# A fused block-sparse attention and SwiGLU kernel: where the later query masks are made, which PSUM bank three tiles use, and what is loaded ahead of the down weights

## The chip, the cores and the metric

The kernel runs on one core of a Trainium2 chip. The metric is the device time of one execution in microseconds, as a median of several runs; lower is better. Besides those runs, one execution was profiled, and all details of where time goes come from it.

Engines are named as in the profile: PE (matrix multiply; PEld is its weight load), DVE (vector), ACT (scalar), POOL (GpSimd), SP (the queue that issues most plain DMAs and the DMA transposes). Each engine runs its instructions in the order of the program, and so do the queues that issue DMAs.

## The reference

```python
# q, k, v: [4, 8, 768, 64]; sampled_blocks: [24, 3]
scores = (q @ k^T) / sqrt(64)
# block mask over 24 blocks of 32: neighbours within 1, first and last block in rows and columns,
# and three sampled key blocks for each query block; outside the mask the score is -1e9
attn = exp(scores - max); attn = attn / sum(attn)
x = (attn @ v)            # heads side by side: [3072, 512]
xn = x / sqrt(mean(x*x) + 1e-6) * rms_g
out = (silu(xn @ w_gate) * (xn @ w_val)) @ w_out      # d_ff = 1536
```

The same mask serves all batches and heads. All heads of a token must be done before its norm and its feed-forward part (FFN) can start.

## The kernel before

**Tiling.** The query columns are cut into groups: batch 0 in three groups of two 128-query chunks, batches 1 to 3 in two groups of three chunks each. For each group the kernel loops over the eight heads: `scores` (L316) multiplies keys by queries into a PSUM tile `st` and lets ACT take the exponential into `ex`; `values` (L332) multiplies `ex` by the values, with a column of ones that gives the row sums; `pv` and `pv_two` (the latter for group 0, two heads in a tile) divide by the sum and write to `stage`. The values of a head are computed one head later than its scores (`late_pv`, L518).

**The mask** is part of the matmul: 24 more rows (`D:KR`) of `KT` hold an indicator of the key's block, and 24 more rows of `QT` hold a large negative number where the block isn't allowed. The rows for the queries of group 0 (`qmask[:, 0:2P]`) are made by DVE at L237. Those for groups 1 and 2 are made by DVE in the middle of group 0: `qnat` at L641, then `mask_queries` twice (L246, L650), and then SP sends them to the other seven heads (L652).

**From a group to its FFN.** When a group's last head is done, `squares` (L364) sums the squares on DVE, `rms_power` (L374) takes the power -0.5 on POOL (`rstd`), `rms_scale` scales rows into `xs` on DVE, and `transpose_x` turns them on PE (`tx`) and copies them to `xg` on DVE. For some later groups a DMA turns them; of group 2 one chunk is turned by PE, in tile `tx3` (L412). Then `ffn_pieces` (L426) makes a list of pieces: 12 gates (`gp`), 12 values (`vp`) and the down parts (`yp`, which read `wo`). The pieces are handed out over the next group's heads at fixed places (`position`, L500), four a head, so PE's order is written out in the program.

**PSUM.** `ps_f` has three banks (tag `ff`) for FFN tiles, fillers and some transposes. `ps_o` has one bank (tag `ot`) for value tiles and other transposes. `ps_s` has two double banks for `st`.

**Loads.** Nearly all loads are issued by POOL, in program order: keys, queries and values of batch 0, with the later query chunks (`load_q0(pr, 2, NC)`, tile `qbf`), `load_gv` for `wg` and `wv` in a first quarter, a second quarter and a half, then `wo` (L636), then from group 1 on batch 1's pairs (`load_qk`, `load_v`, L537). `rms_power` stands in the same queue. Batch 0's keys and queries are turned by PE (`transpose_qk`, tile `tqk`); those of later batches by DMA on SP (`turn`, L297, tile `turned`), and placed by two more DMAs a step later (`place`, L305). For batch 1, `turn` starts with group 2 (L583).

**Fillers.** `keep_busy` (L167) issues matmuls on a constant tile whose result nobody reads.

Of the kernel before, what the change touches and what calls it, by code (L numbers as in the profile page):

```python
# [9 lines left out]
FP32 = mybir.dt.float32  # L10
BF16 = mybir.dt.bfloat16
# [7 lines left out]
def kernel(  # L19
# [17 lines left out]
    nc = tc.nc  # L37
# [100 lines left out]
    rmsg = const.tile([P, NP], FP32, name="rmsg")  # L138
    gain = const.tile([P, DM], FP32, name="gain")

    def first_cast(h, which):
        cols = 2 * D if which else NC * D
        t16 = ld.tile([P, cols], BF16, name="t16", tag=f"t16{which}", bufs=1)
        nc.scalar.copy(out=t16, in_=first[(h, which)][:, 0:cols])
        return t16

    def first_turn(src, which, unread=None):
# [40 lines left out]
    for pr in range(NP):  # L188
        if pr == 0:
            load_q0(1, 0, 2)  # L190
        elif pr + 1 < NP:
            load_one(0, pr + 1, kbf)
            load_q0(pr + 1, 0, 2)
        load_v(0, pr)
        if pr == NP - 2:
            load_q0(0, 2, NC)
    load_gv(0, NF // 4)
    load_q0(1, 2, NC)
    load_gv(NF // 4, NF // 2)

    mhalf = const.tile([P, HC], FP32, name="mhalf")
    nc.vector.memset(mhalf, -0.5)
# [34 lines left out]
    for m, (lo, hi) in enumerate(((0, 6), (6, 11), (11, 16))):  # L237
        nc.vector.tensor_scalar(
            out=qmask.rearrange("p (c i r) -> p c i r", c=NC, r=16)[:, 0:2, :, lo:hi],
            in0=bm[0:NB, :].rearrange("p (i m) -> p i m", m=3)[:, :, m].unsqueeze(1).unsqueeze(  # L240
                3).to_broadcast([NB, 2, 8, hi - lo]),
            scalar1=-MASKV, scalar2=MASKV, op0=ALU.mult, op1=ALU.add)
    mask_keys(0, HC)
    qnat = const.tile([32, S], BF16, name="qnat")

    def mask_queries(third):  # L246

        lo, hi = 2 * third, 2 * third + 2
        nc.vector.tensor_copy(
            out=qmask.rearrange("p (c r) -> p c r", c=NC)[:, lo:hi, :],  # L250
            in_=qnat[0:NB, :].rearrange("p (r c) -> p c r", c=NC)[:, lo:hi, :])

    def copy_rows(T, m, lo, hi, c_lo, c_hi):

        nc.vector.tensor_copy(
# [20 lines left out]


    def transpose_qk(b, pr, which, lo, hi, spare, copy):
# [61 lines left out]
    def pv(grp, h, ex, stage):  # L340
        n = grp[2]
        op = ps_o.tile([P, HC, 80], FP32, name="op", tag="ot")
        values(grp, h, ex, op)
        rz = work.tile([P, HC], FP32, name="rz", tag="rz", bufs=2)
        nc.vector.reciprocal(out=rz[:, 0:n], in_=op[:, 0:n, D])  # L345
        nc.vector.tensor_tensor(  # L346
            out=stage[:, 0:n, h * D:(h + 1) * D], in0=op[:, 0:n, 0:D],
            in1=rz[:, 0:n].unsqueeze(2).to_broadcast([P, n, D]), op=ALU.mult)

    pair_op = {}  # L350

    def pv_two(grp, h, ex, stage):

        if h % 2 == 0:
            pair_op[0] = ps_o.tile([P, 2, 2, 80], FP32, name="op2", tag="ot")
        op = pair_op[0]
        values(grp, h, ex, op[:, h % 2])
        if h % 2 == 0:
            return
        rz = work.tile([P, 2, 2], FP32, name="rz2", tag="rz2", bufs=2)  # L360
        nc.vector.reciprocal(out=rz, in_=op[:, :, :, D])
        nc.vector.tensor_tensor(  # L362
            out=stage[:, 0:2, (h - 1) * D:(h + 1) * D].rearrange("p c (e d) -> p e c d", e=2),
            in0=op[:, :, :, 0:D], in1=rz.unsqueeze(3).to_broadcast([P, 2, 2, D]), op=ALU.mult)  # L364
# [36 lines left out]
    def transpose_x(e, half):  # L401
        xs, xg, n = e["xs"], e["xg"], e["grp"][2]
        if by_dma(e):
            if e["grp"] == groups[FIRST] and half == 2:
                t = ps_o.tile([P, KD, P], BF16, name="tx3", tag="ot")
                for c in range(KD):
                    nc.tensor.transpose(
                        out=t[:, c, :], in_=xs[:, 2, c * P:(c + 1) * P], identity=ident)
                nc.vector.tensor_copy(out=xg[:, :, 2 * P:3 * P], in_=t)
            return  # L410
        if half == 2:
            return  # L412
        pool, tag = (ps_f, "ff") if e["grp"] == groups[0] else (ps_o, "ot")
        t = pool.tile([P, 2, HC, P], BF16, name="tx", tag=tag)
        for w in range(2):
            c = 2 * half + w
            for it in range(n):
                nc.tensor.transpose(  # L418
                    out=t[:, w, it, :], in_=xs[:, it, c * P:(c + 1) * P], identity=ident)
# [87 lines left out]
    waiting = []  # L507
    ending = None

    def after_pv(e, h):  # L510
# [7 lines left out]
    def late_pv():  # L518

        e, h, ex = waiting.pop(0)  # L520
        if e["grp"] == groups[0]:
# [6 lines left out]
                    squares(e, it, (H - 2) * D, H * D)  # L528
                rms_power(e)
        else:  # L530
            pv(e["grp"], h, ex, e["stage"])
            after_pv(e, h)
        return e if h == H - 1 else None

    def side_work(gi, h):

        if gi == 1:  # L537
            if h == 1:
                load_qk(1, 0)
                load_v(1, 0)  # L540
                load_v(1, 1)
                load_qk(1, 1)
            if h == 3:
                nc.gpsimd.dma_start(
                    out=gain, in_=moe_rms_g.unsqueeze(0).to_broadcast([P, DM]))
                load_qk(1, 2)
            if h == 5:
                load_qk(1, 3)
# [41 lines left out]
    TX = 2  # L590

    def begin(grp):
        return {
# [5 lines left out]
    def first_group():  # L599
# [24 lines left out]
        keep_busy(1, 512)  # L624
        copy_rows(KT, kind, 2, 4, 0, S)
        copy_rows(QT, qmask, 2, 4, 0, 2 * P)
        k_turn(1)
        q_turn(1, (act, act))
        keep_busy(1, 512)

        head(1, lambda: keep_busy(1, 512))
# [1 line left out]
        load_q0(2, 2, NC)  # L633
        load_q0(3, 2, NC)
        load_gv(NF // 2, NF)
        nc.gpsimd.dma_start(out=wo, in_=moe_w_out.rearrange("(c p) f -> p c f", p=P))  # L636
        k_turn(2)

        head(2, lambda: q_turn(2))
        late_pv()  # L640
        nc.vector.tensor_scalar(  # L641
            out=qnat[0:NB, :].rearrange("p (a w) -> p a w", w=32),
            in0=bm[0:NB, :].unsqueeze(2).to_broadcast([NB, NB, 32]),
            scalar1=-MASKV, scalar2=MASKV, op0=ALU.mult, op1=ALU.add)
        keep_busy(1, 512)

        head(3)
        late_pv()
        cast_v(0, 1, nc.vector)
        for third in range(1, FIRST):  # L650
            mask_queries(third)
        nc.sync.dma_start(  # L652
            out=QT[0][D:KR, 1:H, 2 * P:S],
            in_=qmask[:, 2 * P:S].unsqueeze(1).to_broadcast([NB, H - 1, S - 2 * P]))
        k_turn(3)
        keep_busy(1, 512)

        head(4, lambda: q_turn(3))
        late_pv()
# [3 lines left out]
        late_pv()  # L663
        cast_v(0, 2, nc.vector)
        transpose_qk(0, 0, 1, 1, HC, True, (dve, dve))
        keep_busy(1, 512)

        head(6)
        late_pv()
# [5 lines left out]
        keep_busy(1, 512)  # L675

        head(7)
        late_pv()
        keep_busy(1, 512)
        late_pv()  # L680
# [2 lines left out]
    for gi, grp in enumerate(groups):  # L683
# [6 lines left out]
        for h in range(H):  # L690
# [42 lines left out]
            if h == 0 and ending is not None:  # L733
                rms_scale(ending, 0)
            if h == H - 1:
                squares(cur, 1, 0, (H - 1) * D)
            waiting.append((cur, h, ex))
    pe = waiting[0][0]
    squares(pe, 2, 0, (H - 1) * D)
# [48 lines left out]
```

## Time and profile before

| | |
|---|---|
| median of 3 runs | 313.87 us (313.78 to 314.47) |
| the profiled execution | 314.58 us, of which the span from first to last instruction is 312.8 us |
| granted TensorE clock | 1.000 |
| PE busy | 302.8 us, 97% |
| DVE, ACT, POOL busy | 202.7, 205.1, 52.9 us |
| DMA, POOL's queue | 17.90 MB |
| DMA, SP's queue | 18.47 MB |
| first values of group 0's FFN (`gp`) | at 27.1 us |
| first down part (`yp`) | at 46.25 us |
| first scores of batch 1 (384 columns) | at 68.6 us |

A row of the profile that names an engine, a line and `out<-in` tells the tiles by the program's names. "x12" counts instructions. In a wait "A <- B", A stood still and B ended that. The end of a matmul is modelled, so a busy PE can still be late.

### The profile page before, as it was taken

The numbers are of one execution on the slowest core, as the hardware profiler recorded it, in microseconds if no ns is written. First come the engines' busy times: TensorE is split into PE (matmuls) and PEld (weight loads), VectorE is DVE, ScalarE is ACT, GpSimd is POOL, SyncE is SP. The second block draws the span as 40 slices with busy tenths as digits, with TensorE's granted clock in tenths as the row PEclk, the third lists the DMA queues.
The fourth block names the chain that finished last, engine by engine and source line by source line (L and its number), as shares of the span: only waits on it lengthen the run. The fifth ranks groups of instructions, "written<-read, shape, count | busy, mean of one in ns | idle before, by whom it ended". The sixth has DMA issues, their size and how long they took to land.

```text
span 312.8 us, 7261 instructions
## 1 busy us (share of the span) xinstructions
PE 302.8 (97%) x2850; PEld 201.1 (64%) x2869; DVE 202.7 (65%) x557; ACT 205.1 (66%) x332; POOL 52.9 (17%) x79
## 2 busy tenths in 40 slices
PE   8888999999999999999999999999999999999996
PEld 5666886976787566655666566655666566655653
DVE  6978875775578647682767457683777636674860
ACT  4976775777788586667676766766767567632331
POOL 9935132100220122012010122010000100010000
PEclk9999999999999999999999999999999999999999
DMA  7999999999789469605784277714000130002002
GB/s 166 271 210 208 208 265 142 175 227 136 209 147 162 104 134 158 141 20 146 149 152 101 70 182 127 143 40 119 34 2 0 36 118 2 1 2 101 2 0 102
DMA packets 66730, 36.84 MB, mean 118 GB/s; under 512 B 48308, under 2 KB 62288, under 8 KB 66696
## 3 DMA queue, kind: packets, MB, share of 16 engines
q0 software_dynamic: 16064, 17.90, 31.7%
q1 hardware_dynamic: 50596, 18.47, 27.7%
q8 instruction: 22, 0.36, 0.5%
q14 instruction: 12, 0.10, 0.1%
q10 hardware_dynamic: 36, 0.01, 0.0%
HBM read 28.59 MB, written 6.29 MB: 112 GB/s over the span
## 4 chain that ended last, share of the span: by engine, by line
PE 86%; DMA 7%; ACT 3%; DVE 2%; issue 1%; SPq 1%; ACTq 0%
PE yp L464 19%; PE gp L436 19%; PE vp L447 18%; PE st L325 18%; PE op L336 11%; DMA turned<-qbf 4%; ACT ex L328 2%; DMA QT<-turned 2%; DMA first<-in_q_dram 1%; PE tx L418 0%; DVE QT L293 0%; DVE junk L369 0%; DVE stage L362 0%; PE tqk L288 0%; SPq L133 0%
## 5 line engine op out<-in xcount | busy, mean ns | idle before, releaser
L328 ACT ACTIVATE ex<-st 128x768 bf16<-128x768 f32 x192 | 153.9, 812 | 56.2 <-PE st L325 54.5
L325 PE MATMUL st<-QT,KT 88*128 88x384 bf16 (+1 forms) x432 | 93.5, 308 | 1.9 <-DMA QT<-turned 0.7
L451 DVE SCALAR_TENSOR_TENSOR u<-th,gp 128x384 bf16<-128x384 bf16 (+1 forms) x108 | 54.8, 508 | 40.7 <-ACT th L440 39.0
L436 PE MATMUL gp<-xg,wg 128*128 128x384 bf16 (+1 forms) x432 | 80.7, 307 | 0.0
L447 PE MATMUL vp<-xg,wv 128*128 128x384 bf16 (+1 forms) x432 | 80.2, 307 | 0.4 <-DVE u L451 0.4
L464 PE MATMUL yp<-wo,hps 128*128 128x512 bf16 (+1 forms) x284 | 71.6, 369 | 0.9
L440 ACT ACTIVATE th<-gp 128x384 bf16<-128x384 f32 (+1 forms) x108 | 48.9, 453 | 28.9 <-PE gp L436 28.7
L453 DVE TENSOR_TENSOR hps<-u,vp 128x384 bf16<-128x384 bf16 (+1 forms) x108 | 55.1, 510 | 11.4 <-PE vp L447 0.3
L325 PEld LDWEIGHTS <-KT 88*128 88x128 bf16 x432 | 41.7, 98 | 27.0 <-issue 1.9
L447 PEld LDWEIGHTS <-wv 128*128 128x128 bf16 x432 | 40.6, 97 | 20.9 <-issue 0.6
L436 PEld LDWEIGHTS <-wg 128*128 128x128 bf16 x432 | 40.2, 97 | 20.3
L336 PEld LDWEIGHTS <-ex 128*128 128x128 bf16 x1152 | 46.0, 98 | 11.2 <-DVE stage L362 0.8
L336 PE MATMUL op<-Vp,ex 128*128 128x65 bf16 x1152 | 48.8, 194 | 1.6 <-DVE stage L362 0.5
L464 PEld LDWEIGHTS <-hps 128*128 128x128 bf16 x300 | 27.7, 97 | 22.4
L377 POOL TENSOR_TENSOR rstd<-ssq,mhalf 128x3 f32<-128x3 f32 (+1 forms) x9 | 7.3, 815 | 139.4 <-DVE ssq L369 139.4
L345 DVE RECIPROCAL rz<-op 128x3 f32<-128x3 f32 (+1 forms) x64 | 11.2, 174 | 26.2 <-PE op L336 26.1
L470 ACT ACTIVATE yo<-yp 128x512 f32<-128x512 f32 (+1 forms) x25 | 14.4, 576 | 16.0 <-PE yp L464 16.0
L99 POOL DMA_DIRECT2D vraw<-in_v_dram x16 | 12.0, 753 | 69.4 <-DVE Vp L118 60.4
L346 DVE TENSOR_TENSOR stage<-op,rz 128x192 bf16<-128x192 f32 (+1 forms) x64 | 21.8, 341 | 2.2
L369 DVE CUSTOM_DVE_ANT_0 junk<-stage 128x448 bf16<-128x448 bf16 (+1 forms) x24 | 14.8, 618 | 0.6
L389 DVE SCALAR_TENSOR_TENSOR xs<-stage,rstd,gain 128x512 bf16<-128x512 bf16 x15 | 10.4, 748 | 4.4 <-POOL rstd L377 4.4
L87 POOL DMA_DIRECT2D kbf<-in_k_dram x15 | 11.1, 742 | 7.0 <-DMA wo<-in_moe_w_out_dram 7.0
(73 smaller groups left out, 104.6 us busy)
## 6 DMA issues: line engine op xcount, KB each, us to landing
vraw<-in_v_dram POOLq DMA_DIRECT2D x16, 384.0 KB, 5.1
out_dram<-yo SPq DMA_DIRECT2D x23, 256.0 KB, 2.2
kbf<-in_k_dram POOLq DMA_DIRECT2D x15, 192.0 KB, 5.8
qbf<-in_q_dram POOLq DMA_DIRECT2D x12, 192.0 KB, 6.0
KT<-turned SPq DMA_DIRECT2D x24, 96.0 KB, 4.2
QT<-turned SPq DMA_DIRECT2D x24, 96.0 KB, 2.3
wo<-in_moe_w_out_dram POOLq DMA_DIRECT2D x1, 1536.0 KB, 20.5
wg<-in_moe_w_gate_dram POOLq DMA_DIRECT2D x2, 384.0 KB, 9.8
```

What stands on the lines that cost most here:

```text
L325: nc.tensor.matmul(out=at[:, e, 0:tg], lhsT=KT[b % 2][0:KR, h, jt * P:(jt + 1) * P], rhs=QT[b % 2][0:KR, h, c0 * P:c0 * P + tg], start=Tru ...
L328: nc.scalar.activation(out=ex[:, nj * part:nj * (part + 1), :], in_=at[:, 0:nj, 0:tg], func=AF.Exp, scale=SCALE)
L336: nc.tensor.matmul(out=op[:, it, 0:VW], lhsT=ex[:, jt, it * P:(it + 1) * P], rhs=Vp[b % 2][:, h, jt, :], start=(jt == 0), stop=(jt == NC - 1))
L346: nc.vector.tensor_tensor(out=stage[:, 0:n, h * D:(h + 1) * D], in0=op[:, 0:n, 0:D], in1=rz[:, 0:n].unsqueeze(2).to_broadcast([P, n, D]), ...
L369: nc.vector.tensor_tensor_reduce(out=junk[:, 0:hi - lo], in0=part, in1=part, scale=1.0, scalar=(e["ssq"][:, it:it + 1] if lo else DM * 1e- ...
L436: nc.tensor.matmul(out=gp[:, 0:tg], lhsT=wg[:, c, f * P:(f + 1) * P], rhs=xg[:, c, 0:tg], start=(c == 0), stop=(c == KD - 1))
L440: nc.scalar.activation(out=th[:, 0:tg], in_=gp[:, 0:tg], func=AF.Tanh, scale=0.5)
L447: nc.tensor.matmul(out=vp[:, 0:tg], lhsT=wv[:, c, f * P:(f + 1) * P], rhs=xg[:, c, 0:tg], start=(c == 0), stop=(c == KD - 1))
L451: nc.vector.scalar_tensor_tensor(out=u[:, 0:tg], in0=th[:, 0:tg], scalar=1.0, in1=gp[:, 0:tg], op0=ALU.add, op1=ALU.mult)
L453: nc.vector.tensor_tensor(out=hps[:, f, 0:tg], in0=u[:, 0:tg], in1=vp[:, 0:tg], op=ALU.mult)
L464: nc.tensor.matmul(out=yp, lhsT=hps[:, f, tt * P:(tt + 1) * P], rhs=wo[:, f, lo:hi], start=(f == 0), stop=(f == NF - 1))
L470: nc.scalar.mul(out=yo, in_=yp, mul=0.5)
```

## The change

- The masks of the later queries are made by POOL, early, into a tile of their own (`later`), two thirds of three instructions each; they stand in POOL's queue between batch 0's loads and the first `load_gv`. SP sends them to all eight heads, ahead of the small load of `rmsr`. `qnat` and DVE's copies are gone.
- The cast of the second head's queries (`first_cast(1, 1)`) goes from ACT to DVE, a little later.
- `load_q0(1, 2, NC)` goes ahead of `load_gv`. `load_qk(1, 0)`, the first key and query pair of batch 1, goes from group 1 to just ahead of `wo`.
- `op2` of group 0's last two heads and `tx3` go to a bank of `ps_f`. The last values of group 0 are computed between the two score parts of group 1's first head, in place of a filler.
- The rest of the queries of pair 1 is turned at the end of group 0 and not at head 0 of group 1. The order of `q_turn(1)` and `k_turn(1)` is swapped. Four more fillers are left out.
- The normalisation of group 1's head 0 is put behind `transpose_x` on DVE (`held_back`). The squares of group 1 are taken in two halves for two of its chunks (`halves`).
- `turn` for batch 1 starts at head 5 of group 1 (`TURN`).

```diff
-        if pr == NP - 2:
-            load_q0(0, 2, NC)
-    load_gv(0, NF // 4)
-    load_q0(1, 2, NC)
-    load_gv(NF // 4, NF // 2)
+        if pr >= NP - 2:
+            load_q0(pr - NP + 2, 2, NC)
...
+    def mask_queries(third, dst, eng):
+        at = [0] + [-(-(32 * m - 2 * third) // NC) for m in (1, 2)] + [16]
+        for m in range(3):
+            lo, hi = at[m], at[m + 1]
+            eng.tensor_scalar(
+                out=dst.rearrange("p (c i r) -> p c i r", c=2, r=16)[:, :, :, lo:hi],
+                in0=bm[0:NB, :].rearrange("p (i m) -> p i m", m=3)[:, :, m].unsqueeze(
+                    1).unsqueeze(3).to_broadcast([NB, 2, 8, hi - lo]),
+                scalar1=-MASKV, scalar2=MASKV, op0=ALU.mult, op1=ALU.add)
+
+    mask_queries(0, qmask[:, 0:2 * P], nc.vector)
+    later = const.tile([32, S - 2 * P], BF16, name="later")
+    for third in range(1, FIRST):
+        mask_queries(third, later[0:NB, 2 * P * (third - 1):2 * P * third], nc.gpsimd)
+    load_gv(0, NF // 4)
+    load_gv(NF // 4, NF // 2)
     mask_keys(0, HC)
...
-    second16 = [first_cast(1, which) for which in range(2)]
+    second16 = [first_cast(1, 0, nc.scalar.copy)]
...
+    nc.sync.dma_start(
+        out=QT[0][D:KR, :, 2 * P:S],
+        in_=later[0:NB, :].unsqueeze(1).to_broadcast([NB, H, S - 2 * P]))
     nc.sync.dma_start(out=rmsr, in_=moe_rms_g.rearrange("(h p) -> h p", p=P))
...
+    second16.append(first_cast(1, 1, nc.vector.tensor_copy))
...
-            pair_op[0] = ps_o.tile([P, 2, 2, 80], FP32, name="op2", tag="ot")
+            pool, tag = (ps_f, "ff") if h == H - 2 else (ps_o, "ot")
+            pair_op[0] = pool.tile([P, 2, 2, 80], FP32, name="op2", tag=tag)
...
-                t = ps_o.tile([P, KD, P], BF16, name="tx3", tag="ot")
+                t = ps_f.tile([P, KD, P], BF16, name="tx3", tag="ff")
...
     def after_pv(e, h):
+        if halves(e) and h in (H // 2, H // 2 + 1):
+            squares(e, h - H // 2, 0, H // 2 * D)
         if h == H - 2:
-            squares(e, 0, 0, (H - 1) * D)
+            squares(e, 0, H // 2 * D if halves(e) else 0, (H - 1) * D)
...
-                load_qk(1, 0)
+                load_qk(1, 1)
                 load_v(1, 0)
                 load_v(1, 1)
-                load_qk(1, 1)
...
-        if gi == 1 and h in (0, 2, 4):
-            transpose_qk(0, h // 2 + 1, 1, 1, HC, h == 0, (dve, dve))
+        if gi == 1 and h in (2, 4):
+            transpose_qk(0, h // 2 + 1, 1, 1, HC, False, (dve, dve))
...
-        if gi == FIRST - 1:
-            turn(1, h // 2, h % 2)
+        at = (gi - 1) * H + h - TURN
+        if gi < FIRST and 0 <= at < H:
+            turn(1, at // 2, at % 2)
...
         load_gv(NF // 2, NF)
+        load_qk(1, 0)
         nc.gpsimd.dma_start(out=wo, in_=moe_w_out.rearrange("(c p) f -> p c f", p=P))
...
         head(7)
+        transpose_qk(0, 1, 1, 1, HC, True, (dve, dve))
         late_pv()
...
                     transpose_x(ending, 1)
+                    held_back.pop()()
                     enter(ending, NPOS + 4)
                     ending = None
-            if thin:
+            after_turn = gi == 1 and h == 0
+            if after_turn:
+                ending = late_pv()
+            elif thin:
                 keep_busy(1, 512)
             position()
             scores(grp, h, 1, ex)
...
-            last = late_pv()
-            if last is not None:
-                ending = last
+            if not after_turn:
+                last = late_pv(gi == 1 and h == 1)
+                if last is not None:
+                    ending = last
```

More of the change, by code (lines that the diff above doesn't have):

```diff
@@ L139, with first_cast @@
     gain = const.tile([P, DM], FP32, name="gain")
-    def first_cast(h, which):
+    def first_cast(h, which, copy):
         cols = 2 * D if which else NC * D
         t16 = ld.tile([P, cols], BF16, name="t16", tag=f"t16{which}", bufs=1)
-        nc.scalar.copy(out=t16, in_=first[(h, which)][:, 0:cols])
+        copy(out=t16, in_=first[(h, which)][:, 0:cols])
         return t16
@@ L234 @@
             op0=ALU.is_equal, op1=ALU.max)
[L237 to L242, printed above, removed]
-    mask_keys(0, HC)
[L244 to L251, printed above, removed]
+    def mask_queries(third, dst, eng):
[13 more added lines that the diff above has]
+    load_gv(NF // 4, NF // 2)
+    mask_keys(0, HC)
     def copy_rows(T, m, lo, hi, c_lo, c_hi):
@@ L343, in pv, with normalise @@
         values(grp, h, ex, op)
[L344 to L348, printed above, removed]
+        def normalise():
+            rz = work.tile([P, HC], FP32, name="rz", tag="rz", bufs=2)
+            nc.vector.reciprocal(out=rz[:, 0:n], in_=op[:, 0:n, D])
+            nc.vector.tensor_tensor(
+                out=stage[:, 0:n, h * D:(h + 1) * D], in0=op[:, 0:n, 0:D],
+                in1=rz[:, 0:n].unsqueeze(2).to_broadcast([P, n, D]), op=ALU.mult)
+        return normalise
     pair_op = {}
@@ L508, with halves @@
     ending = None
+    def halves(e):
+        return e["grp"] == groups[1]
     def after_pv(e, h):
+        if halves(e) and h in (H // 2, H // 2 + 1):
+            squares(e, h - H // 2, 0, H // 2 * D)
         if h == H - 2:
-            squares(e, 0, 0, (H - 1) * D)
+            squares(e, 0, H // 2 * D if halves(e) else 0, (H - 1) * D)
         if h == H - 1:
@@ L516, in after_pv, with late_pv @@
             rms_power(e)
-    def late_pv():
+    held_back = []
+    def late_pv(hold=False):
         e, h, ex = waiting.pop(0)
@@ L530, in late_pv @@
         else:
-            pv(e["grp"], h, ex, e["stage"])
-            after_pv(e, h)
+            normalise = pv(e["grp"], h, ex, e["stage"])
+            if hold:
+                held_back.append(normalise)
+            else:
+                normalise()
+                after_pv(e, h)
         return e if h == H - 1 else None
@@ L590 @@
     TX = 2
+    TURN = 5
     def begin(grp):
@@ L623, in first_group @@
                 first_copy(1, which, second[which], w, dve)
-        keep_busy(1, 512)
         copy_rows(KT, kind, 2, 4, 0, S)
         copy_rows(QT, qmask, 2, 4, 0, 2 * P)
+        q_turn(1, (act, act))
         k_turn(1)
-        q_turn(1, (act, act))
         keep_busy(1, 512)
@@ L640, in first_group @@
         late_pv()
[L641 to L644, printed above, removed]
         keep_busy(1, 512)
@@ L649, in first_group @@
         cast_v(0, 1, nc.vector)
[L650 to L654, printed above, removed]
         k_turn(3)
-        keep_busy(1, 512)
         head(4, lambda: q_turn(3))
@@ L665, in first_group @@
         transpose_qk(0, 0, 1, 1, HC, True, (dve, dve))
-        keep_busy(1, 512)
         head(6)
@@ L674, in first_group @@
                                 op0=ALU.mult)
-        keep_busy(1, 512)
         head(7)
+        transpose_qk(0, 1, 1, 1, HC, True, (dve, dve))
         late_pv()
@@ L735 @@
             if h == H - 1:
-                squares(cur, 1, 0, (H - 1) * D)
+                squares(cur, 1, H // 2 * D if halves(cur) else 0, (H - 1) * D)
             waiting.append((cur, h, ex))
```

## The prediction

> **What bounds the kernel now.** I read the page first, then PE's waits, then the timeline of POOL with the landings of the tiles it loads, then PE's timeline where the first group hands over to the FFN, and last the DMA rate by stretches.
>
> ```profile
> PE 302.8 (97%) x2850; PEld 201.1 (64%) x2869; DVE 202.7 (65%) x557; ACT 205.1 (66%) x332; POOL 52.9 (17%) x79
> ```
>
> PE is the bound, and its stream is in program order, so a change can gain only what PE now stands idle or does for nothing. PE's waits, from the trace (total, times, longest):
>
> ```profile
> PE st L325 <- DMA QT<-turned: 0.7, 1, 0.7
> PE st L325 <- DVE QT L293: 0.6, 1, 0.6
> PE op L336 <- DVE stage L362: 0.5, 1, 0.5
> PE op L336 <- DVE xg L409: 0.5, 1, 0.5
> PE vp L447 <- DVE u L451: 0.4, 1, 0.4
> ```
>
> These five are 2.7 us, and each is a target of the change. The ends of matmuls are modelled, so the loss from start to start is a little more: 0.9 for the first (at 68 us) and 0.7 for the `xg` one (at 107 us). Both lie late, alone on PE's path. The `DVE QT` and `stage` waits lie at 20 to 25 us, the `u` wait at 43 us.
>
> The loads are the second thing to look at. POOL's timeline (start, duration, form, wait before it), and then the landing times of `wg`, `wv` and `wo` from their tile views:
>
> ```profile
> 10.40 0.85 POOL L109 DMA_DIRECT2D wg<-in_moe_w_gate_dram  x1
> 13.31 0.77 POOL L109 DMA_DIRECT2D wg<-in_moe_w_gate_dram  x1
> 16.20 0.80 POOL L109 DMA_DIRECT2D wg<-in_moe_w_gate_dram  x1
> 19.41 0.74 POOL L109 DMA_DIRECT2D wv<-in_moe_w_val_dram  x1 [2.41 <-DMA wg<-in_moe_w_gate_dram]
> 22.10 1.02 POOL L636 DMA_DIRECT2D wo<-in_moe_w_out_dram  x1 [1.95 <-DMA wv<-in_moe_w_val_dram]
> 24.55 0.73 POOL L377 TENSOR_TENSOR rstd<-ssq,mhalf 128x2 f32<-128x2 f32 x1 [1.44 <-DVE ssq L369]
> ...
> 42.85 0.70 POOL L87 DMA_DIRECT2D kbf<-in_k_dram  x1 [6.96 <-DMA wo<-in_moe_w_out_dram]
> ```
>
> ```profile
> DMA to landing us min/median/max: 8.7/10.9/15.1
> ...
> DMA to landing us min/median/max: 10.6/12.1/15.6
> ...
> DMA to landing us min/median/max: 20.5/20.5/20.5
> ```
>
> Count POOL's DMAs in program order. The first `wg` is number 12 and lands at 10.40 + 8.7 = 19.1; number 20 (`wv`) is let go at 19.41. The first `wv`, number 13, was issued at 11.22 and lands at 21.8; number 21 (`wo`) is let go at 22.10. `wo` lands at 42.6; number 29 (`kbf`) is let go at 42.85. So POOL's DMA number n waits for the landing of number n-8, plus 0.3 us, and all behind it on POOL waits too. The second `wg` (number 15) lands at 13.31 + 10.9 = 24.2.
>
> PE at the hand-over, and the first use of `wo`, from the timeline:
>
> ```profile
> 25.32 0.77 DVE L397 TENSOR_SCALAR xs<-stage,rstd 128x512 bf16<-128x512 bf16 x2
> ...
> 26.15 0.56 PE L418 MATMUL tx<-ident,xs 128*128 128x128 bf16 x7 [0.19 <-DVE xs L397]
> ...
> 46.25 0.81 PE L464 MATMUL yp<-wo,hps 128*128 128x512 bf16 x2
> ```
>
> Last, the windows (width, busy by engine, clock, DMA share, GB/s) before and after the first batch-1 transpose, and that transpose on SP's timeline:
>
> ```profile
> 36.00:42.00 6.00, 5.97 (x78) 5.18 (x76) 4.58 (x14) 4.94 (x10) 0.00 (x0) 1.00 1.25 213
> ...
> 47.00:52.00 5.00, 5.00 (x50) 3.11 (x48) 2.35 (x8) 3.08 (x5) 1.92 (x3) 1.00 1.71 113
> ```
>
> ```profile
> 43.60 1.32 SPq L301 DMA_TRANSPOSE turned<-kbf  x1
> ...
> 53.86 2.61 SPq L310 DMA_DIRECT2D KT<-turned  x2
> ```
>
> The transpose is issued the moment its `kbf` is there, and its placing goes out 10 us later. Meanwhile the DMA rate falls from 208 to 213 GB/s (all of 24 to 42 us) to 113, with loads still queued.
>
> **Step 1, the first group (to 25 us): gains that are covered.** DVE sheds `qnat` (0.54) and two copies (0.67), and takes one cast (about 0.3, from the ACT rows of L144). PE sheds five 512-column fillers at 0.21 us (three `yp` matmuls of that width take 0.65 in the chain). The bank move and the earlier `tqk` take away the `stage` and `QT` waits. Together PE would be through with group 0 some 1.9 us earlier, and `ssq`, now 24.5, would be ready at 22.6. Against this: the six mask instructions on POOL do not stand in the trace. The nearest POOL rows are 0.29 (select, 128x128) and 0.73 (the power); with 24 partitions and 80 to 96 elements I take 0.4, so 2.4 us (1.7 to 4.4), ending at 13.7 instead of 11.25 (12.9 to 15.7). The loads behind them do not suffer: before the first `wg` the queue still has `vraw` and `qbf` to move until about 16. SP's mask DMA waits for these masks, and `rmsr`, issued at 6.77 today, now stands behind it, issued at about 14.7; `trms` on PE needs it at 18 or so. Group 1's first scores, due at about 20, now take head 0's mask from that DMA as well. Landings on SP run from 3.3 us (`first`) upwards, so PE stalls at one of the two for 0 to 3 us. All of this has up to 2.9 us of cover in step 2 and I cost it at nothing; without that cover it would be what rival C says.
>
> **Step 2, `rstd` behind `wo`.** The two loads put ahead of `wo` make it number 23, so it waits for number 15, the second `wg`: 24.2 + 0.3 = 24.5. Its issue takes 1.02, and `rms_power` of group 0 stands behind it on POOL: 25.5 + 0.73 = 26.3. `xs` follows at 26.35, and the bulk of `tx` 0.83 after that, as today (25.32 to 26.15): 27.2 instead of 26.15, **+1.0**. Behind `xs` on DVE wait only `xg` and the held normalisation, which the next values need just about then. The exponentials are further ahead when PE resumes (-0.2). Of the `u` wait I take -0.2, since a 192-column square is shorter than the 448-column one (0.62) and two more are paid at heads 4 and 5, where DVE is busy 8 us in 10. The first `yp` then falls due at 46.25 + 0.6 = 46.85.
>
> **Step 3, `wo` lands later.** 384 KB more in front of it at 208 GB/s: 42.6 + 1.9 = 44.5. But `kbf` and `qbf` of the first pair are now there at 36 and 37 us, SP has nothing else to wait for, and two transposes go out into the stream of `wo`. What one costs is bounded by two rows. Above: in 47 to 52 us 565 KB moved, 192 of them the transpose's own, so 670 KB of loads are missing, 3.2 us. Below: the `vraw` issued at 88.88, beside the transpose of 88.65, landed 4.5 us later, not over the page's median of 5.1, so nothing. I take 2.2, nearer to the upper row because the queue is as deep as there: 44.5 + 4.4 = 48.9, a stall of 48.9 - 46.85 = **+2.05** (0 to 4.1).
>
> **Step 4, the later waits.** The transposes of batch 1 are three heads earlier, so `QT<-turned` is no wait any more: **-0.9**. `tx3` in an FFN bank: **-0.6** of 0.7. Group 1's `rstd` stands behind `qbf` of pair 3, number 32, which now waits for number 24, a load behind `wo`; that shifts with the stall, nothing net.
>
> **Sum.** 1.0 - 0.4 + 2.05 - 1.5 = +1.15 on a span of 312.8: 313.95. The profiled execution took 314.58, 0.7 over the median 313.87; on the median the forecast is **315.0**. A measurement of this kernel can tell about 0.2% (0.63 us) from no change.
>
> **Rivals.**
> - **A, the forecast** (`rstd` held, `wo` late): 315.0, chance 0.42.
> - **B, `wo` in time: faster.** If a transpose costs only its own bytes, 192 KB at 208 GB/s = 0.9 us, `wo` lands at 44.5 + 1.9 = 46.4, before 46.85. Then 0.6 - 1.5 = -0.9: 313.0. It decides where a transpose costs under 1.2 us. For it: the `vraw` at 88.88. Against it: 113 GB/s. Chance 0.28. The Trainium skill, "DMA: Bandwidth & Descriptors", section on queues, rings and completion order, says that each DMA engine takes turns between its queues packet by packet; by that rule the transpose would take just its share and B would be right. The window at 47 us disagrees.
> - **C, neither holds.** If `rstd` follows `ssq` 1.9 us earlier and the transposes cost nothing, the first `yp` is due at 46.25 - 1.9 - 0.4 = 43.95, starts with `wo` at 44.5 (-1.75), and step 4 adds -1.5: 310.7. Against it: three waits out of three follow n-8. Chance 0.10.
> - **D, the full price twice:** `wo` at 50.9, a stall of 4.1: 317.0. Chance 0.15.
> - **E, the clock.** PE now stands still for some 2.7 us before `tx` and 2 at `wo`, with fewer fillers; the longest gap today is 0.9. At the start the 256-column fillers take 0.21 us each (ten in 2.31), until about 5 us; later matmuls of that width take 0.11. If PE fell back to that for as long again, some 4 us, it would cost 2.0 on top of A: 317.0. Chance 0.05. The Trainium skill, "TensorE: Matmul & The Clock Gate", part 1, says that an idle window of about 3.4 us halves the clock; no run here shows it.
>
> **Numbers.** Faster by over 0.2%: C, 0.23 of B, 0.03 of A, 0.36. Within: 0.05 of B and 0.08 of A, 0.13. Slower: 0.51. The range 311.5 to 317.0 leaves out most of C and the upper half of D and E. A by itself runs from 313.6 to 316.2, by the bounds of `wo` between 47.5 and 50.1.
>
> **What would show it.** Step 2: `wo` issued at about 24.5 with a wait on `wg` before it, `rstd` right behind, `tx` at 27 with some 2.7 us of idle PE. Step 3: a wait of `yp` on `wo`, and a DMA rate well below 208 GB/s between 39 and 48 us. Step 4: no wait on `QT<-turned`, nor of `op` on L409. Wrong would be `rstd` before 25, or a first `yp` before 46.5.

## The result, and the profile after

The changed kernel takes 324.18 us (median of 6 runs, 323.53 to 324.8) against 313.84 for the kernel before, measured beside it on the same chip: a ratio of 1.0326 (95% interval 1.031 to 1.0341), slower. The forecast was 315.0, in a range up to 317.0. The profiled execution took 324.39 us with a span of 322.6, so 9.8 more than the span before. Single runs of f4 (322.23 us) and g3 (322.0 us) below were disturbed, and the ratios leave them out.

The page's first part, after (busy, share of the span, instructions):

```profile
PE 307.4 (95%) x2864; PEld 202.6 (63%) x2864; DVE 202.1 (63%) x559; ACT 204.9 (64%) x331; POOL 54.7 (17%) x85
```

PE is busy 4.6 us longer, and its share fell from 97% to 95%: it stands still more, and what it does takes longer. PE's waits, after (total, times, longest, us):

```profile
PE tx L425 <- DVE stage L351: 7.0, 1, 7.0
PE trms L680 <- DMA rmsr<-in_moe_rms_g_dram: 1.5, 1, 1.5
```

Of the five waits that were targets, four are gone, and `vp` on `u` is down to 0.2. One wait of 7.0 us costs more than all five did. It names DVE's `stage`, which was ready long before; what came last is found one engine further. POOL's timeline, after (start, duration, form, wait ahead of it):

```profile
23.81 1.02 POOL L655 DMA_DIRECT2D wo<-in_moe_w_out_dram  x1 [0.98 <-DMA wg<-in_moe_w_gate_dram]
26.04 0.73 POOL L384 TENSOR_TENSOR rstd<-ssq,mhalf 128x2 f32<-128x2 f32 x1 [1.21 <-DVE ssq L376]
...
54.50 0.72 POOL L87 DMA_DIRECT2D qbf<-in_q_dram  x1 [17.92 <-DMA turned<-qbf]
55.22 0.72 POOL L87 DMA_DIRECT2D kbf<-in_k_dram  x1
55.93 0.72 POOL L87 DMA_DIRECT2D qbf<-in_q_dram  x1
56.66 0.72 POOL L384 TENSOR_TENSOR rstd<-ssq,mhalf 128x2 f32<-128x2 f32 x1
```

The query load of batch 1's pair 2 stands still for 17.92 us until a transpose has landed. That is no wait for its own data. Query tiles share four buffers, and this load was given the one of batch 1's first query tile, which the transpose was still reading (e1 below tests this). Behind it in POOL's order stand both loads of pair 3 and group 1's `rstd`, at 56.66. In the kernel before, `rstd` and the first `tx` that needs it stood here:

```profile
46.92 0.71 POOL L377 TENSOR_TENSOR rstd<-ssq,mhalf 128x2 f32<-128x2 f32 x1 [0.18 <-DVE ssq L369]
...
49.88 0.39 PE L418 MATMUL tx<-ident,xs 128*128 128x128 bf16 x4
```

The transpose of the first query tile and its placing on SP's timeline, after, then what waits on DVE and PE:

```profile
37.09 3.44 SPq L304 DMA_TRANSPOSE turned<-qbf  x1
...
53.98 1.27 SPq L313 DMA_DIRECT2D QT<-turned  x2
```

```profile
57.42 0.70 DVE L404 TENSOR_SCALAR xs<-stage,rstd 128x512 bf16<-128x512 bf16 x2 [8.15 <-POOL rstd L384]
```

```profile
47.82 0.81 PE L471 MATMUL yp<-wo,hps 128*128 128x512 bf16 x3
...
58.57 0.61 PE L425 MATMUL tx<-ident,xs 128*128 128x128 bf16 x4 [6.96 <-DVE stage L351]
58.98 1.49 PE L471 MATMUL yp<-wo,hps 128*128 128x512 bf16 x3
```

Batch 1's first transpose (keys), issued at 35.65, is placed 10.8 us later; the second, issued at 37.09, 16.9 later, beside a stream of loads. `rstd`, `xs` and `tx` follow one another. And the three `yp` matmuls take 1.49 us at 58.98 where they took 0.81 at 47.82. The windows show the clock (width, busy of the five engines' columns, granted clock, DMA share, GB/s):

```profile
18.00:20.00 2.00, 0.50 (x10) 0.35 (x7) 0.87 (x2) 0.71 (x2) 1.17 (x1) 0.93 1.32 207
20.00:23.00 3.00, 3.00 (x30) 2.35 (x30) 1.21 (x5) 1.51 (x2) 1.41 (x2) 0.50 1.31 202
...
52.00:56.00 4.00, 0.00 (x0) 0.00 (x0) 0.00 (x0) 0.62 (x1) 1.50 (x3) 0.73 1.36 122
56.00:61.00 5.00, 2.43 (x11) 1.42 (x12) 1.67 (x6) 0.00 (x0) 2.65 (x4) 0.50 1.22 203
```

Twice PE stands idle and is then granted half its clock: after the 1.5 us wait at 18 us, and after the 7.0 us wait.

Landmarks on PE's timeline tell where the difference arises. Starts in us, to 0.01; the columns from e1 on are experiments told below:

| landmark | before | after | e1 | e3 | e4 | g1 | f3 | f4 |
|---|---|---|---|---|---|---|---|---|
| first `tx` (group 0) | 25.72 | 27.21 | 26.96 | 25.76 | 26.19 | 26.00 | 26.29 | 24.85 |
| first `yp` | 46.24 | 47.81 | 47.57 | 46.22 | 48.06 | 46.64 | 48.01 | 45.46 |
| group 1's `tx` | 49.88 | 58.57 | 51.23 | 58.18 | 51.70 | 50.28 | 51.65 | 49.09 |
| group 2's `tx` | 76.21 | 86.72 | 80.65 | 83.80 | 79.58 | 76.21 | 77.25 | 75.28 |
| group 3's `tx` | 106.66 | 117.16 | 111.37 | 114.25 | 110.02 | 106.67 | 107.70 | 105.73 |
| last `tx` | 282.11 | 291.91 | 286.29 | 290.15 | 285.86 | 282.14 | 282.45 | 280.49 |
| last matmul | 309.48 | 319.29 | 313.66 | 317.52 | 313.23 | 309.51 | 309.82 | 307.86 |

After against before: 1.57 us late at the first `yp`, 8.69 at group 1's `tx`, 10.51 at group 2's, and 9.81 at the end. So 1.57 arise in the first group, 7.12 in the stall, 1.82 net between the two `tx`, and 0.70 is won back behind group 3's `tx`. These are places on PE's path in two executions, not what each mend alone would bring: e2 takes away the first wait, and the end stays.

### The profile page after: what moved, and what is told of

The parts are those of the page before. It is cut to its first block, busy times and chain, and to the rows that moved or that the text cites. A ratio compares the mean times of both kernels' runs of the same rounds, so it can differ in the third digit from the quotient of the medians.

```text
span 322.6 us, 7280 instructions
## 1 busy us (share of the span) xinstructions
PE 307.4 (95%) x2864; PEld 202.6 (63%) x2864; DVE 202.1 (63%) x559; ACT 204.9 (64%) x331; POOL 54.7 (17%) x85
## 4 chain that ended last, share of the span: by engine, by line
PE 84%; DMA 7%; POOL 4%; DVE 2%; issue 1%; ACT 0%; SPq 0%; POOLq 0%
PE yp L471 19%; PE gp L443 19%; PE vp L454 18%; PE st L328 17%; PE op L339 10%; DMA turned<-qbf 5%; DMA rmsr<-in_moe_rms_g_dram 2%; POOL kbf L87 1%; POOL vraw L99 1%; PE tx L425 1%; POOL q L80 1%; DVE junk L376 1%; DVE xs L404 0%; POOL rstd L384 0%; POOL qbf L80 0%
## 5 line engine op out<-in xcount | busy, mean ns | idle before, releaser
L328 PE MATMUL st<-QT,KT 88*128 88x384 bf16 (+1 forms) x432 | 94.9, 311 | 0.7 <-ACT ex L331 0.4
L471 PE MATMUL yp<-wo,hps 128*128 128x512 bf16 (+1 forms) x300 | 75.7, 377 | 0.0
L447 ACT ACTIVATE th<-gp 128x384 bf16<-128x384 f32 (+1 forms) x108 | 48.9, 453 | 29.1 <-PE gp L443 28.9
L339 PEld LDWEIGHTS <-ex 128*128 128x128 bf16 x1152 | 46.9, 99 | 10.1 <-issue 1.0
L339 PE MATMUL op<-Vp,ex 128*128 128x65 bf16 x1152 | 49.6, 195 | 0.4 <-DVE Vp L118 0.2
L351 DVE TENSOR_TENSOR stage<-op,rz 128x192 bf16<-128x192 f32 (+1 forms) x64 | 21.8, 341 | 2.2
L376 DVE CUSTOM_DVE_ANT_0 junk<-stage 128x448 bf16<-128x448 bf16 (+2 forms) x24 | 14.4, 600 | 0.5
L396 DVE SCALAR_TENSOR_TENSOR xs<-stage,rstd,gain 128x512 bf16<-128x512 bf16 x15 | 10.4, 748 | 4.4 <-POOL rstd L384 4.4
L87 POOL DMA_DIRECT2D qbf<-in_q_dram x12 | 8.7, 721 | 19.5 <-DMA turned<-qbf 17.9
## 6 DMA issues: line engine op xcount, KB each, us to landing
wo<-in_moe_w_out_dram POOLq DMA_DIRECT2D x1, 1536.0 KB, 22.4
```

The lines of the kernel that those rows point to most:

```text
L328: nc.tensor.matmul(out=at[:, e, 0:tg], lhsT=KT[b % 2][0:KR, h, jt * P:(jt + 1) * P], rhs=QT[b % 2][0:KR, h, c0 * P:c0 * P + tg], start=Tru ...
L339: nc.tensor.matmul(out=op[:, it, 0:VW], lhsT=ex[:, jt, it * P:(it + 1) * P], rhs=Vp[b % 2][:, h, jt, :], start=(jt == 0), stop=(jt == NC - 1))
L351: nc.vector.tensor_tensor(out=stage[:, 0:n, h * D:(h + 1) * D], in0=op[:, 0:n, 0:D], in1=rz[:, 0:n].unsqueeze(2).to_broadcast([P, n, D]), ...
L376: nc.vector.tensor_tensor_reduce(out=junk[:, 0:hi - lo], in0=part, in1=part, scale=1.0, scalar=(e["ssq"][:, it:it + 1] if lo else DM * 1e- ...
L447: nc.scalar.activation(out=th[:, 0:tg], in_=gp[:, 0:tg], func=AF.Tanh, scale=0.5)
L471: nc.tensor.matmul(out=yp, lhsT=hps[:, f, tt * P:(tt + 1) * P], rhs=wo[:, f, lo:hi], start=(f == 0), stop=(f == NF - 1))
```

## Experiments

All are edits of the changed kernel, but for f2. "Before" is the kernel before, timed beside each. Part one of the change is the masks with the loads and casts around them, part two the PSUM banks, and part three batch 1's first pair ahead of `wo` with the transposes that start earlier (`TURN`).

**e1, the buffers in turn.** Each query tile takes the next of four buffers; pair 2's load then gets one that an early PE transpose has read.

```
+    def q_tile():
+        taken[0] += 1
+        return ld.tile([P, 2, NC * D], BF16, name="qbf", tag=f"qbf{taken[0] % 4}", bufs=1)
...
-            t = ld.tile([P, 2, NC * D], BF16, name="qbf", tag="qbf", bufs=4)[:, :, lo * D:]
+            t = q_tile()[:, :, lo * D:]
...
```

> The changed kernel with one edit: the four buffers of the query tiles are handed out in turn, so that batch 1's third query load takes the buffer of batch 0's third rest load (as in the kernel before) and not that of batch 1's first. Theory 1 (the buffer): the third query load then waits for no transpose, group 1's rstd is on time, the 7.0 us wait of tx on DVE's stage is gone and with it some 3 us of half clock behind it; 324.2 - 10 = 314.2 us, 313.2 to 315.2, tx of group 1 at about 51.6 us. Theory 2 (the transposes beside the load stream): the transpose still lands at 54, and the load traffic stays late; something else of group 1 waits as long, the time stays above 320 us. Theory 3 (the early stall at 18 us is the loss, the wait at 51 us only shows it): over 322 us.

Measured: 318.44 us, ratio 1.0145 (1.0095 to 1.0195). Group 1's `tx` came at 51.23, as theory 1 says, with no half clock after it, but the time came down by 5.7 us only. Theory 3 falls. Theory 1 was incomplete, and theory 2 holds a part: PE's waits now begin with

```profile
PE st L334 <- DMA QT<-turned: 1.7, 1, 1.7
```

and SP's timeline and the windows of e1 show a second collision:

```profile
48.18 4.21 SPq L310 DMA_TRANSPOSE turned<-kbf  x1
...
67.25 1.27 SPq L319 DMA_DIRECT2D KT<-turned  x2
```

```profile
62.00:66.00 4.00, 4.00 (x56) 3.63 (x55) 3.09 (x9) 3.19 (x7) 0.73 (x1) 1.00 1.33 83
```

With the load of pair 2 let go, the loads of pair 3 and the mask copies run from 46.6 us beside pair 1's transposes. The key transpose of pair 1, issued at 48.18, is placed at 67.25, 19 us later, and the rate falls to 83 GB/s at a DMA share as high as ever (1.33). Batch 1's first scores wait for something else in this stretch, the placing of pair 0's queries. From the chains that ended last, e1 and then the kernel before (start, us):

```profile
54.57 16.23 DMA QT<-turned
```

```profile
62.70 5.67 DMA QT<-turned
```

It goes out 8.1 us earlier than in the kernel before and lands 2.4 us later. In the profiled execution of e1, `trms` doesn't wait for `rmsr`. Its first group is late all the same: PE waits 1.14 us for a `kbf` of batch 0 at 10.8 us and then has a clock of 0.50 for some 3.4 us.

**e2, `rmsr` first**, and **e4, both edits.** `rmsr`'s load goes ahead of the mask DMA for the later queries.

```
+    nc.sync.dma_start(out=rmsr, in_=moe_rms_g.rearrange("(h p) -> h p", p=P))
     nc.sync.dma_start(
         out=QT[0][D:KR, :, 2 * P:S],
...
-    nc.sync.dma_start(out=rmsr, in_=moe_rms_g.rearrange("(h p) -> h p", p=P))
```

> The changed kernel with the load of rmsr issued on SP ahead of the mask DMA for the later queries; the buffers as in the changed kernel. Theory 1: PE's 1.5 us wait at 18 us and the half clock behind it (19.9 to 23.1 us) go, the first yp comes some 1.5 us earlier (46.3 instead of 47.8), but rstd of group 1 is still let go by the transpose that lands at about 54 us, so the end stays: 323.5 to 324.4 us. Theory 3: the gain carries through to the end, 322.0 to 322.8 us or less.

> The first and second edits together: buffers handed out in turn and rmsr loaded ahead of the mask DMA. Theory 1: what the second edit saves is no longer covered, so this is 1.0 to 1.6 us under the first edit alone: 312.8 us (312.0 to 313.8). If rstd of group 0 is then held by the issue of wo at 23.8 (step 2 of the prediction), rstd at about 24.9 and the gain is 1.1 of the 1.6 at most. Rival: the first edit's run has other cover (wo's landing at 46.2 or later), the gain is 0 to 0.4 us.

Measured: e2 324.61 us, ratio 1.0332 (1.0309 to 1.0354), no gain; e4 318.76, ratio 1.0129 (1.0061 to 1.0198), no gain over e1 either, where 312.8 us had been expected. That e2's end is set by the stall is as theory 1 says. But the first `yp`, expected at 46.3 in e2, came at 47.84, and at 48.06 in e4. The wait on `rmsr` is gone; in its place stands step 2 of the prediction, `rstd` behind `wo`. POOL and the windows of e2:

```profile
23.89 1.02 POOL L655 DMA_DIRECT2D wo<-in_moe_w_out_dram  x1 [0.94 <-DMA wg<-in_moe_w_gate_dram]
24.93 0.75 POOL L384 TENSOR_TENSOR rstd<-ssq,mhalf 128x2 f32<-128x2 f32 x1
```

```profile
24.00:26.00 2.00, 0.00 (x0) 0.00 (x0) 0.28 (x2) 0.81 (x1) 1.67 (x2) 1.00 1.35 204
...
27.00:30.00 3.00, 3.00 (x23) 2.03 (x21) 1.26 (x6) 1.20 (x2) 1.89 (x3) 0.50 1.16 210
```

PE is 2.2 us idle until `tx` at 26.13, and the half clock of 20 to 23 us has moved to 27 to 30.

**e3, the stall filled.** Idle matmuls keep PE busy through it.

```
                 if gi == 1:
                     transpose_x(ending, 1)
...
+                if gi == 2:
+                    keep_busy(32, 512)
                 transpose_x(ending, 0)
```

> The changed kernel with 32 idle matmuls of 512 columns (some 6.9 us at full clock) put on PE ahead of group 1's first transposes, where PE stands idle for 7.0 us; no other edit. If the half clock after the idle stretch (0.50 from 56 to 64 us) is a cost of its own: clock 1.00 there, three yp matmuls 0.81 us instead of 1.49, and 321.2 us (320.6 to 322.0). If the low clock costs nothing (something else limits there): 324.2 us, and above if the fillers delay tx.

Measured: 323.20 us, ratio 1.0286 (1.0263 to 1.031). The clock stayed at 1.00, and from group 1's `tx` to group 2's it took 25.62 us in place of 28.15: the half clock costs 2.5 us there. Of that, 1.15 us were lost again between the `tx` of group 3 and the last one; there `gp` waits twice for `xg` (0.35 us before 153.38, 0.48 before 225.75), which after's profile lacks. The median moved by about 1 us, less than expected; whether these waits belong to the edit or to that execution stays open. In this execution PE waited for `rmsr` for 0.58 us only, without a half clock behind it, and the first `yp` came at 46.22; the edit doesn't touch that part.

**f1 and f4, without the third part**, with the buffers in turn (f1), and `rmsr` first as well (f4).

```
         load_gv(NF // 2, NF)
-        load_qk(1, 0)
         nc.gpsimd.dma_start(out=wo, ...
...
-    TURN = 5
+    TURN = 8
```

(and `load_qk(1, 0)` back at head 1 of group 1.)

> The changed kernel with its buffers handed out in turn (as in e1) and without its third part: batch 1's first pair is loaded behind wo, at head 1 of group 1, and the transposes start with group 2 (TURN = 8), as in the kernel before. Parts one and two stay. Theory 1 (the loss left in e1 comes from the transposes of batch 1 on SP running beside the loads on POOL, each slowing the other, so that the later ones land late for batch 1's first scores): QT<-turned is again one wait of 0.7 to 0.9 us, the DMA rate between 62 and 66 us is near 195 GB/s and not 83, group 2's tx comes 26.3 us after group 1's and not 29.4. What stays is 1.35 us of lateness at group 1's tx from the first group (rmsr), less 0.6 for tx3: 314.6 us (314.0 to 315.4). Rival (the loss left in e1 comes from parts one and two): 317 to 319 us.

> As f1, and rmsr loaded ahead of the mask DMA. Parts one and two of the change with their early stall mended: group 0's rstd no longer waits for the half clock of 19.9 to 23.1 us; 1.0 to 1.5 us under f1, 313.3 us (312.5 to 314.0), which would be under the kernel before. If group 0's rstd is covered by something else than rmsr (DVE's own queue), it stays at f1's 314.6.

Measured: f1 313.87 us, ratio 0.9989 (0.9976 to 1.0002), as fast as before; f4 313.05, ratio 0.9967 (0.9952 to 0.9981), faster than before. Theory 1 holds in the main: what e1 and e4 lost beside the stall belongs to the third part. f1 is a little under its range. Its rate between 62 and 66 us is 237 GB/s, group 2's `tx` comes 25.60 us after group 1's, and the wait on `QT<-turned` that was expected is not there. f4 is 0.82 us under f1, a little less than expected. How `rmsr` makes that difference, f1's profiled execution doesn't show: it has no wait on `rmsr`, and its first group is late by waits for batch 0's loads at 10 to 12 us with a clock of 0.50 behind them. With part three gone, `wo` is issued at 20.05 in f4 (20.12 in f1), and `rstd` waits for its data alone:

```profile
23.68 0.73 POOL L390 TENSOR_TENSOR rstd<-ssq,mhalf 128x2 f32<-128x2 f32 x1 [2.61 <-DVE ssq L382]
```

**f2, the third part alone**, on the kernel before, buffers in turn.

> The kernel before with the third part alone (batch 1's first pair loaded ahead of wo, TURN = 5), the query buffers handed out in turn, so that no load waits for a transpose. Theory 1: the transposes beside the load stream make group 2 late by some 3 us, less little for QT<-turned: 316.5 to 318.5 us, with a DMA rate of 80 to 140 GB/s somewhere between 58 and 70 us. Rival (the prediction's step 4: the transposes three heads earlier save the wait on QT<-turned, 0.9 us; the wo load is in time as in the changed kernel): 312.5 to 314 us.

Measured: 318.31 us, ratio 1.013 (1.008 to 1.0181), theory 1. The four runs lie between 316.84 and 319.84, and the profiled one is the slowest. PE's first two waits in it:

```profile
PE st L331 <- DMA QT<-turned: 3.0, 2, 2.0
PE tx L424 <- DVE stage L352: 1.6, 1, 1.6
```

The wait on `QT<-turned`, 0.7 us in the kernel before and meant to go, is 3.0 us. The wait of `tx` is again one for `rstd`, at 50.89: ahead of it stands pair 3's `qbf`, number 32, let go at 50.15, after number 24 (26.30 + 23.3 = 49.6).

**f3, the loads as changed, the transposes as before.** e4 with `TURN = 8`.

> The changed kernel with both mends of e4 (buffers in turn, rmsr ahead of the mask DMA) and the transposes of batch 1 started with group 2 (TURN = 8) as in the kernel before, while its first pair still loads ahead of wo. If the start of the transposes is what costs (theory 1): no transpose runs in the stream of wo, 36 to 46 us are at 208 GB/s, wo lands at about 44.5 and k of pair 3 is let go 1.5 us earlier; 313.3 us (312.7 to 314.3). If the order of the loads is what costs: 316 to 318.5 us, as e4.

Measured: 315.5 us, ratio 1.0038 (1.0014 to 1.0062), between the two. Against e4 the later start is worth 3.3 us; against f4 the order of the loads costs 2.45. The landmarks place the second: f3 is 1.44 behind f4 at the first `tx` (`rstd` behind `wo`'s issue at 24.06) and 2.55 at the first `yp`, where PE, 1.9 us idle before `tx`, had a clock of 0.50 from 27 to 30 us. `wo` itself landed at 46.1, 2 us before its first use.

**g1, `rstd` ahead of the waiting load.** Buffers as in the changed kernel, so the load still waits; but it and pair 3's loads are issued behind `rstd`.

```
-                load_qk(1, 2)
-            if h == 5:
-                load_qk(1, 3)
+                load_one(1, 2, kbf)
         if gi == 2 and h == 1:
+            load_one(1, 2, qbf)
+            load_qk(1, 3)
```

> The changed kernel with its own buffers (batch 1's third query tile still waits for the transpose of its first), but that load and the two of pair 3 stand behind group 1's rstd in POOL's program, at head 1 of group 2 in place of heads 3 and 5 of group 1. If the stall comes from what is queued behind the waiting load on POOL: rstd at 49 to 50 us, group 1's tx at 51.2 us in place of 58.6, no half clock after it, and the load itself still let go at about 54; 316 to 319 us, as e1 or a little better, since the loads of pair 2 and 3 then run later. If the load's lateness itself is what costs (batch 1's pair 2 and 3 missing at its scores), the wait moves to the scores of group 3 and the time stays at 322 us or more.

Measured: 314.93 us, ratio 1.001 (0.9982 to 1.0038). POOL's timeline:

```profile
47.15 0.71 POOL L384 TENSOR_TENSOR rstd<-ssq,mhalf 128x2 f32<-128x2 f32 x1 [9.80 <-DVE ssq L376]
54.77 0.74 POOL L87 DMA_DIRECT2D qbf<-in_q_dram  x1 [6.91 <-DMA turned<-qbf]
```

The load is let go at 54.77, as in the changed kernel, by the same transpose, and no engine waits for what it loads: group 1's `tx` comes at 50.28, group 2's at 76.21, as in the kernel before. This settles the main cause: not the late load, but `rstd` queued behind it. The time is better than expected. The loads that run beside pair 1's transposes in e1 are held back here, and that key transpose, issued at 48.81, is placed at 57.60 and not at 67.25.

**g2, `tx3` back in its bank**, and **g3, one head earlier** (f4 with `TURN = 7`).

> f4 (parts one and two, buffers in turn, rmsr first) with the transposes tx3 of the first group of batch 1 back in a bank of the values' pool, as in the kernel before. By step 4 of the prediction op then waits 0.7 us for xg's copy again at about 107 us, and the time is 0.6 us over f4: 313.7 us. If the wait had only moved in f4: no difference, 313.1 us.

> f4 with the transposes of batch 1 started one head earlier (TURN = 7). If starting them earlier harms only by the loads that they run beside (k and q of pairs 2 and 3 and the mask copies, on their way until about 56 us): the second transpose goes out at 44 us and not at 50, lands after 53 with the DMA rate between 44 and 56 us lower than f4's, and group 2's tx comes 0.5 to 2.5 us later: 313.5 to 315.5 us. If instead each head earlier saves of the wait on QT<-turned (0.75 us in f4), 312.3 us.

Measured: g2 314.48 us, ratio 1.0012 (0.9986 to 1.0039). The wait of `op` on `xg` is back, and from group 3's `tx` to the last it takes 175.44 us against f4's 174.76: 0.68, as step 4 has it. The rest of the difference to f4 in the profile is a wait on `QT<-turned` of 1.7 us against 0.6, which the edit doesn't touch. g3: 317.27 us, ratio 1.0063 (1.0013 to 1.0113), beyond the expected harm; by the two ratios, one head earlier costs 1% or 3 us over f4. The wait in its profile:

```profile
PE st L334 <- DMA QT<-turned: 2.5, 1, 2.5
```

It is followed by a clock of 0.57 from 71 to 75 us, a loss that the forecast didn't have. The second transpose, issued 4.7 us earlier than in f4, is placed at 61.87 (61.26 in f4), and its placing then takes 7.82 us (5.54). The rate between 50 and 58 us was 142 GB/s; f4's was 219 and 187 in the two halves of that stretch.

**h1, f4 with g1's move.**

> f4 (parts one and two, buffers in turn, rmsr first) with g1's move: the query load of batch 1's pair 2 and both of pair 3 stand behind group 1's rstd, at head 1 of group 2. The loads that run beside batch 1's first transposes are then fewer until 50 us. If that lets the second transpose land earlier (f4: about 61), the 0.75 us wait on QT<-turned of f4 goes: 312.3 us (311.8 to 312.9). If the transposes are as late as in f4 whatever loads stand beside them: 313.1 us, and above it if pair 2 or 3 now comes late for its scores.

Measured: 313.54 us, ratio 0.9985 (0.9973 to 0.9998), not better than f4. The second transpose was placed at 60.39 (61.26 in f4), but the placing took 6.66 us (5.54 in f4), and the scores of batch 1 still waited for 0.7 us (0.6). f4 stays the best version.

## Why the prediction was wrong

The sum of the four steps was +1.15 us; the span grew by 9.8. That the change is slower was forecast, but neither of the two terms that made the forecast slower, `tx` held by `wo` and a stall of `yp` on `wo`, is what slowed it; that the direction agrees is luck. Measured, it reads 1.57 (first group) + 7.12 (stall) + 2.53 (half clock behind it, from e3) - 0.71 (the rest of that stretch: after's 28.15 between the `tx` of groups 1 and 2, less 2.53, against 26.33) - 0.70 (`tx3`) = 9.81.

- **The step that failed is in step 4:** "Group 1's `rstd` stands behind `qbf` of pair 3, number 32, which now waits for number 24 ...; that shifts with the stall, nothing net." The queue was right, and so was the wait of number n for n-8: number 24 landed at 48.5 (26.74 + 21.8; 48.1 in e1, where `rstd` then ran at 49.41), and that alone costs little: from the first `yp` to group 1's `tx` it takes 3.66 us in e1, 3.64 in the kernel before; only in f2, where number 24 landed at 49.6, does `tx` wait 1.6 us for it. But number 30 two places ahead had a second wait, for its buffer. The prediction followed the loads by number and did not ask which buffer each would get. The profile before gave no sign of it: its two late `qbf` loads, at 31.82 and 46.03, follow the landings of number 19 (16.20 + 15.1 = 31.3) and number 24 (26.70 + 18.8 = 45.5), though their rows name PE. This term, set at nothing, was 7.1 us, and with the half clock 9.7, by the profiles.
- **Step 1, "I cost it at nothing":** the stall on `rmsr` is 1.5 us, inside the 0 to 3 given; the cover failed, since the half clock that follows it was not in the sum. The masks themselves took 1.46 us, less than the 2.4 of the estimate. But this loss is not in every execution: with the same first group, PE waited 0.58 us in e3 and 0.42 in g1, without a half clock, and the first `yp` came at 46.22 and 46.64 (forecast 46.85). Of the six runs of the changed kernel, three have a mean clock of 0.979 and three of 0.983 to 0.984, with medians of 324.39 and 323.79 us; a stretch of 0.50 as long as that of 20 to 23 us is a difference of 0.005. The bulk of `tx` came at 27.63 against the 27.2 of the forecast, but by luck, not for step 2's reason: `rstd` at 26.04 waited for `ssq`, not for `wo`.
- **Step 2, `rstd` behind `wo`:** hidden by step 1's stall in the profiled execution, and real where that stall is small or mended. In e2 `wo` went at 23.89 (forecast 24.5), `rstd` right behind it and `tx` at 26.13. In g1 and e3 the first `tx` is 1.15 and 0.91 us behind f4's without a half clock (forecast +1.0); in f3 it is 1.44, and 2.55 at the first `yp` with the half clock.
- **Step 3, `wo` late:** no stall. `wo` was 22.4 us on its way (20.5 before) and landed at 46.2, not 48.9: 1.7 us over the 44.5 of the bytes alone, where the forecast added 4.4. That is rival B's size (1.8 for two). With one transpose in that stream, in f3, it landed at 46.1, so the price of a single one is not told apart. Where the first group is not late, `wo` is just in time: in g1 the first `yp`, at 46.64, waits 0.3 us for it. The row of 113 GB/s does not tell what a transpose takes from the loads. Both were slow there: the transposes issued at 43.60 and 50.87 landed after 10.2 and 11.2 us, the four loads issued from 42.85 to 46.03 after 8.5 to 10.4.
- **Step 4, -0.9 and -0.6:** `tx3` gave 0.70. The 0.9 of `QT<-turned` is no gain of earlier transposes: that wait grows to 3.0 us in f2 and 1.7 in e1, where the placing of pair 0's queries lands late. In the changed kernel it is gone beside a stall that puts off the scores. Of the runs with earlier transposes and without the stall only g1, with the loads out of the way, keeps a part: 25.93 us between the `tx` of groups 1 and 2 against 26.33 before, 0.4.
- **Rival E, the clock (0.05):** its mechanism was there, at 2.5 us behind the 7.0 us stall; the gap before `tx` that E named made it too, in e2, e4 and f3, though not in e3 and g1. It deserved more than 0.05.

That parts one and two together gain, with `rmsr` first, is shown by f4: 0.33% by the ratio, 1.62 us at the last matmul of the two profiles. How the 0.87 us of it that are there at the first `tx` divide between the masks and the banks was not tried.

## What to carry over

When loads move, ask for each one three things: which load number lets it go, which tile's buffer it will be given and who reads that last, and what small instruction stands behind it in the same queue. A load may well wait 7 us, as in g1, if nothing short that others need is queued behind it. And a DMA that is started earlier, into a stream of loads, can end later, as the placing of pair 0's queries did in e1: price what the stream does to the transposes and their placings, too.

## What was not expected of the hardware

- **DMA transposes and placings in a stream of loads.** The first two transposes of batch 1 (one pair's keys or queries each) landed 10.2 and 11.2 us after their issue in the kernel before, 10.8 and 16.9 in after, and 10.5 and 16.7 in e1; over all batches the medians are 3.5 (keys) and 4.1 us (queries) in the kernel before. In e1 the third was placed 19 us after its issue, in g1, where the loads beside it were held back, 8.8; and e1's placing of pair 0's queries took 16.2 us, against 5.7 in the kernel before. That other loads are the reason is suggested by g1 and not tested alone. The rate fell to 83 GB/s (e1) while the DMA engines' busy share stayed at 1.33.
- **The clock can fall after short gaps too.** PE got a clock of 0.50 for about 3.4 us after waits of 1.1 us (e1, at 10.8 us), 1.5 (after, at 18 us), 1.7 (e4, at 26 us), 1.9 (f3), 2.2 (e2) and 2.5 (g3), but kept 1.00 after waits of 1.3 in g3 (at 11 us), 1.7 in e1 (at 71 us) and g2, and 1.6 and 2.0 in f2. Between 1.1 and 2.0 us the length alone didn't decide. The Trainium skill, "TensorE: Matmul & The Clock Gate", part 1, gives a free-running window of about 3.4 us. The stretches of 0.50 after short gaps agree with its length: the one in after runs from about 19.7 to 23.1 us.
